# Two PSUM banks for attention's values and two for its scores, in place of one and three

## The chip, the core and the metric

The kernel runs on one core of a Trainium2 chip. The metric is the device time of one execution in microseconds (us); lower is better. Three runs of the kernel before gave a median of 904.16 us (903.74 to 908.43).

## What is computed

Three layers follow each other: causal attention with a bias that decays with the distance, a gated feed-forward layer (here "moe"), and a mixer that works first across the positions and then across the channels.

```python
B, H, S, D = 4, 8, 576, 64               # batches, heads, positions, width of a head
scores = q @ k.T / sqrt(D) + minimum(-(cum[:, None] - cum[None, :]), 0)   # cum = cumsum(max(s, 0)); causal
attn   = softmax(scores) @ v
x      = attn as (B, S, 512)
xk, xr = mu_k * x + (1 - mu_k) * x_prev, mu_r * x + (1 - mu_r) * x_prev
x      = sigmoid(xr @ w_r) * (maximum(xk @ w_k, 0) ** 2 @ w_v)
u      = x + (maximum(x.T @ w_tok1, 0) @ w_tok2).T
out    = u + maximum(u @ w_ch1, 0) @ w_ch2
```

## The kernel before

Attention has three stages. **early** (L302) takes the first 256 queries of the eight heads of batch 0. **late** (L348) takes the remaining 320 queries of these heads, with `late_pv` (L375) for their values. The 24 **visits** are the heads of batches 1 to 3, one visit a head, each with `scores` (L267), `transposes` (L389) and `values` (L427). Early and late multiply in plain fp32; the visits split each number into two fp32r parts.

All three go through the same steps for a block of 128 queries. TensorE (PE) multiplies queries and keys into a **score tile** `s` in PSUM (L308; L358; L277 and L278, which add two halves). VectorE (DVE) reads this tile once, adds the mask, writes it to SBUF as `P` and keeps the row's extremum `mx` (L252); from then on the score tile's bank is free. ScalarE (ACT) takes the exponential (L262), DVE the reciprocal of the sum (L263, L264), GpSimd (POOL) scales (L265). PE transposes `P` into a tile `t` (L316, L367, L399), which ACT and DVE copy out as `T`, `PF` or `PT`. PE multiplies that with the values into a **values tile** `pv` in PSUM (L326, L385, L447), which leaves by a copy on DVE (L77) in early and late, and in a visit by a copy on ACT (L453, into `tmp`) and an addition on DVE (L454, into `xt`). A block of 64 queries over 576 keys needs two score tiles of 288 columns. A visit has two values tiles, one for the first 256 queries (from `PF`) and one for the other 320 (from `PT`). The score tiles number 16, 32 and 144 in the three stages.

The feed-forward layer runs beside attention as units of 12 or 24 matmuls (`h` by `up` L467, `r` by `gate` L482, `vd` by `down` L494, all recorded at L109), so that PE has other work while a block waits for DVE, ACT and POOL. Their tiles have two PSUM banks of their own, `ps_d`. The weights are loaded as `raw` (L543) and split on ACT, DVE and POOL (L75, L555 to L561). From 455 us on the rest of the feed-forward layer and the mixer (`c`, `t`, `yn`) run alone.

No order is written out by hand. Each piece has a place (`at(...)`), and a scheduler lays the instructions of every engine in one fixed order when the program is built, from the places and from its own timeline, in which a tile can only be written once a bank of its pool is free. On the chip each engine then works through its own row and waits at its head. SyncE (SP) issues most transfers, also in such a row. PSUM has 8 banks: `ps_d` two, and during attention

```python
        ps_s = att.enter_context(tc.tile_pool(name="ps_s", bufs=3, space=PSUM, reuse_waits="tile"))
        ps_t = att.enter_context(tc.tile_pool(name="ps_t", bufs=2, space=PSUM, reuse_waits="tile"))
        ps_v = att.enter_context(tc.tile_pool(name="ps_v", bufs=1, space=PSUM, reuse_waits="tile"))
```

(L119 to L121). So score tile n uses the bank of tile n-3 and waits for its L252, and every values tile waits until the one before it has been read out.

Of the kernel before, what the change touches and what calls it, by code (L numbers as in the profile page):

```python
# [15 lines left out]
PSUM = bass.MemoryType.PSUM  # L16
# [8 lines left out]
def attention_moe_mixer(  # L25
# [86 lines left out]
    att = ExitStack()  # L112
    with tc.using_default_side("right"):
        qk_p = att.enter_context(tc.tile_pool(name="qk", bufs=1, reuse_waits="tile"))
        p_p = att.enter_context(tc.tile_pool(name="p", bufs=1, reuse_waits="tile"))
        pt_p = att.enter_context(tc.tile_pool(name="pt", bufs=1, reuse_waits="tile"))
        v_p = att.enter_context(tc.tile_pool(name="v", bufs=1, reuse_waits="tile"))
        st_p = att.enter_context(tc.tile_pool(name="st", bufs=6))
        ps_s = att.enter_context(tc.tile_pool(name="ps_s", bufs=3, space=PSUM, reuse_waits="tile"))  # L119
        ps_t = att.enter_context(tc.tile_pool(name="ps_t", bufs=2, space=PSUM, reuse_waits="tile"))  # L120
        ps_v = att.enter_context(tc.tile_pool(name="ps_v", bufs=1, space=PSUM, reuse_waits="tile"))  # L121

    HL = qk_p.tile([128, 4 * S], F32, name="HL")
    VS = v_p.tile([128, NS, 2 * D], F32, name="VS")
# [813 lines left out]
```

## Time and profile before

| | us |
|---|---|
| median of three runs (lowest to highest) | 904.16 (903.74 to 908.43) |
| the profiled execution | 905.17 |
| its span, first to last instruction | 903.4 |
| PE busy in the span | 861.6 |
| DVE, ACT, POOL busy | 515.1, 464.8, 318.5 |

The profile is of one execution. PE and PEld are TensorE's matmuls and its weight loads, which overlap; each matmul here has a weight load of its own. An engine's idle time is put down to what ended it.

### The profile page before, as it was taken

What the parts mean: (1) busy time and instruction counts of PE and PEld (TensorE: products, weight loads), DVE (VectorE), ACT (ScalarE), POOL (GpSimd) and SP (SyncE); (2) the same over time, 40 slices, a digit from 0 to 9 for tenths busy, and PEclk for the clock granted to TensorE, in tenths of its full rate; (3) what the DMA queues carried; (4) which work ended last, traced back from release to release, by engine and by line L of the source; (5) the groups of instructions that cost most, each with busy time, mean ns of one, the idle gap of its engine ahead of it and who ended that gap; (6) DMA issues with size and microseconds to landing.
All of it is one profiled execution on the core that took longest, in us unless ns stands there. A gap on an engine that the chain in (4) does not pass through costs nothing.

```text
span 903.4 us, 16007 instructions
## 1 busy us (share of the span) xinstructions
PE 861.6 (95%) x5456; PEld 789.6 (87%) x5456; DVE 515.1 (57%) x1542; ACT 464.8 (51%) x1264; POOL 318.5 (35%) x463
## 2 busy tenths in 40 slices
PE   6679999999899999999999998999999999999998
PEld 4335678998789989989989998999999999999998
DVE  5687786777898587876657865871331212212120
ACT  4787876766786756758456774760320201112010
POOL 4555535644564535655144764550000000000000
PEclk9759999999999999999999999999999999999999
DMA  7973345456654336542032656564022020211100
GB/s 168 215 193 89 88 124 133 98 122 152 139 117 107 88 81 142 121 108 48 29 118 78 216 160 200 183 180 129 24 75 66 18 79 27 63 43 53 36 1 36
DMA packets 65089, 93.69 MB, mean 104 GB/s; under 512 B 7424, under 2 KB 45568, under 8 KB 65008
## 3 DMA queue, kind: packets, MB, share of 16 engines
q1 hardware_dynamic: 58560, 77.00, 33.1%
q0 software_dynamic: 4576, 15.08, 5.5%
q10 hardware_dynamic: 1872, 0.59, 0.3%
q8 instruction: 43, 0.70, 0.3%
q14 instruction: 38, 0.31, 0.1%
HBM read 56.11 MB, written 14.75 MB: 78 GB/s over the span
## 4 chain that ended last, share of the span: by engine, by line
PE 77%; DMA 8%; DVE 7%; ACT 3%; issue 2%; POOL 2%; SPq 0%; ACTq 0%; POOLq 0%; DVEq 0%
PE c L109 33%; PE vd L109 9%; PE h L109 9%; PE r L109 5%; PE t L109 5%; PE pv L447 4%; PE t L399 3%; PE s L358 3%; PE s L277 2%; PE pv L385 2%; PE s L278 2%; DMA X<-HL 2%; DMA raw<-in_moe_w_k_dram 1%; PE t L367 1%; DVE raw L556 1%
## 5 line engine op out<-in xcount | busy, mean ns | idle before, releaser
L784 ACT ACTIVATE HID<-c 128x384 fp32r<-128x384 f32 x72 | 35.4, 491 | 220.6 <-PE c L109 220.5
L265 POOL TENSOR_SCALAR P<-P,sum 64x576 f32<-64x576 f32 (+4 forms) x160 | 106.5, 670 | 113.9 <-DVE sum L264 58.5
L109 PE MATMUL h<-XK,WK 128*128 128x256 f32 (+1 forms) x768 | 122.9, 301 | 3.6 <-DVE XK L465 1.5
L109 PE MATMUL vd<-KK,WV 128*128 128x256 f32 (+1 forms) x768 | 119.3, 299 | 0.0
L109 PEld LDWEIGHTS h<-XK,WK 128*128 128x128 f32 x768 | 105.6, 188 | 7.9 <-DVE XK L465 2.1
L262 ACT ACTIVATE P<-P,mx 64x576 f32<-64x576 f32 (+4 forms) x160 | 95.8, 600 | 30.7 <-DVE mx L252 26.7
L109 PEld LDWEIGHTS vd<-KK,WV 128*128 128x128 f32 x768 | 105.8, 188 | 2.2 <-ACT raw L555 0.4
L109 PE MATMUL c<-HID,WV 128*128 128x384 f32 x576 | 104.9, 336 | 0.0
L109 PE MATMUL c<-U,WK 128*128 128x384 f32 x576 | 104.2, 337 | 0.5 <-DVE HID L785 0.5
L109 PEld LDWEIGHTS c<-U,WK 128*128 128x128 f32 x576 | 99.9, 188 | 1.1 <-DVE HID L785 0.8
L109 PEld LDWEIGHTS c<-HID,WV 128*128 128x128 f32 x576 | 100.7, 188 | 0.0
L252 DVE CUSTOM_DVE_ANT_0 P<-s,maskc 64x288 f32<-64x288 f32 (+4 forms) x160 | 75.0, 474 | 26.3 <-PE t L399 6.9
L785 DVE SCALAR_TENSOR_TENSOR HID<-c,HID 128x384 fp32r<-128x384 f32 x72 | 40.0, 556 | 87.0 <-ACT HID L784 86.9
L842 DVE TENSOR_TENSOR ut<-c,ut 128x384 f32<-128x384 f32 x24 | 13.4, 558 | 124.1 <-PE c L109 124.1
L477 POOL TENSOR_TENSOR KK<-k,KK 128x256 fp32r<-128x256 f32 (+1 forms) x64 | 54.1, 848 | 31.5 <-ACT k L476 31.2
L109 PE MATMUL r<-XR,WR 128*128 128x320 f32 (+1 forms) x384 | 60.0, 298 | 0.0
L556 DVE SCALAR_TENSOR_TENSOR raw<-raw 128x256 int32<-128x256 int32 (+2 forms) x85 | 47.1, 556 | 19.6 <-ACT raw L555 15.7
L75 ACT ACTIVATE raw<-raw 128x256 f32<-128x256 f32 (+2 forms) x101 | 46.9, 465 | 19.6 <-DMA raw<-in_moe_w_v_dram 6.6
L399 PE MATMUL t<-ident,P 128*128 128x128 f32 (+1 forms) x360 | 53.6, 262 | 2.1 <-DVE PT L425 1.6
L109 PE MATMUL c<-HID,WR 128*128 128x384 f32 x288 | 54.2, 336 | 0.0
L109 PEld LDWEIGHTS r<-XR,WR 128*128 128x128 f32 x384 | 53.0, 188 | 0.7
L109 PE MATMUL c<-U,C1A 128*128 128x384 f32 x288 | 52.9, 343 | 0.0
(111 smaller groups left out, 1627.6 us busy)
## 6 DMA issues: line engine op xcount, KB each, us to landing
X<-HL SPq DMA_DIRECT2D x72, 288.0 KB
raw<-in_moe_w_ch_dram POOLq DMA_DIRECT2D x48, 256.0 KB, 3.3
HL<-in_qk_dram SPq DMA_DIRECT2D x12, 576.0 KB
ut<-u_d SPq DMA_DIRECT2D x32, 192.0 KB
yt<-y_d SPq DMA_DIRECT2D x16, 288.0 KB
u_d<-yt SPq DMA_DIRECT2D x16, 288.0 KB
raw<-in_moe_w_k_dram SPq DMA_DIRECT2D x8, 512.0 KB
raw<-in_moe_w_v_dram SPq DMA_DIRECT2D x16, 256.0 KB
```

Source lines behind the costliest of these rows:

```text
L75: nc.scalar.activation(out=out, in_=in_, func=AF.Copy, scale=scale)
L109: nc.tensor.matmul(ps, a, b, start=first and i == 0, stop=last and i == n - 1)
L252: nc.vector.tensor_tensor_reduce(out=P[0:m, c0:c1], in0=ps[0:m, 0:c1 - c0], in1=maskc[0:m, 512 - q0 + c0:512 - q0 + c1], scale=-scale, sca ...
L262: nc.scalar.activation(out=P[0:m, 0:w], in_=P[0:m, 0:w], func=AF.Exp, bias=mx[0:m, x:x + 1], scale=-1.0, accum_out=sm[0:m, 0:1])
L265: nc.gpsimd.tensor_scalar(out=P[0:m, 0:w], in0=P[0:m, 0:w], scalar1=sm[0:m, 1:2], scalar2=1.0, op0=ALU.mult, op1=ALU.mult)
L358: nc.tensor.matmul(ps[0:m, 0:c1 - c0], x[0:D + 4, 0, q0:q0 + m], x[0:D + 4, 1, c0:c1], start=True, stop=True)
L399: nc.tensor.transpose(ps[0:r, p0 + m * k:p0 + m * k + m], P[0:m, 128 * k:128 * k + r], ident[0:m, 0:m])
L447: nc.tensor.matmul(ps[:, o:n], vv[0:r, k, :], pair[t], start=(k == 0 and t == 0), stop=(k == nk - 1 and t == 1),)
L477: nc.gpsimd.tensor_tensor(out=kk[:, 1, m, 0:n], in0=t[:, 0:n], in1=f32(kk[:, 0, m, 0:n]), op=ALU.subtract)
L556: nc.vector.scalar_tensor_tensor(out=low, in0=high, scalar=3, in1=low, op0=ALU.logical_shift_left, op1=ALU.bitwise_or)
L784: nc.scalar.activation(out=hi, in_=ps, func=AF.Relu)
L785: nc.vector.scalar_tensor_tensor(out=lo, in0=ps, scalar=0.0, in1=f32(hi), op0=ALU.max, op1=ALU.subtract)
```

## The change

Two numbers of buffers: the pool of the score tiles goes from 3 to 2, the pool of the values tiles from 1 to 2. The sum stays 8 banks, and no instruction is added or taken away.

```diff
-        ps_s = att.enter_context(tc.tile_pool(name="ps_s", bufs=3, space=PSUM, reuse_waits="tile"))
+        ps_s = att.enter_context(tc.tile_pool(name="ps_s", bufs=2, space=PSUM, reuse_waits="tile"))
         ps_t = att.enter_context(tc.tile_pool(name="ps_t", bufs=2, space=PSUM, reuse_waits="tile"))
-        ps_v = att.enter_context(tc.tile_pool(name="ps_v", bufs=1, space=PSUM, reuse_waits="tile"))
+        ps_v = att.enter_context(tc.tile_pool(name="ps_v", bufs=2, space=PSUM, reuse_waits="tile"))
```

Score tile n now waits for the L252 of tile n-2, a values tile for the one two before it. Since the scheduler lays its rows by free banks, the rows of all five engines come out anew (on PE 1390 rows of equal instructions before, 1422 after). Three places follow, in the rows as they stand.

Place A is SP's row at the end of the early stage, as a difference. `X_425`, `X_428`, `X_431` and `X_434` are the operands of the first four late heads, loaded from `in_qk_dram` and from `ext_d` (the bias).

```order
 L337 DMA X_431<-in_qk_dram 64x1152
 L343 DMA VV_437<-in_v_dram 128x4x128
 L344 DMA VV_437<-in_v_dram 64x128
-L337 DMA X_434<-in_qk_dram 64x1152
 L343 DMA VV_440<-in_v_dram 128x4x128
-L344 DMA VV_440<-in_v_dram 64x128
 L338 DMA X_425<-ext_d 4x1152
 L338 DMA X_428<-ext_d 4x1152
 L338 DMA X_431<-ext_d 4x1152
+L344 DMA VV_440<-in_v_dram 64x128
+L543 DMA raw<-in_moe_w_v_dram 128x2x256 x2
+L208 DMA HL<-in_qk_dram 128x2x576
```

The load of the fourth head's operand and the second part of a value load went behind the first three biases, which so moved up by two transfers. Transfers from SP take eight semaphores in turn, so each waits until the one eight before it has landed: the first bias used to wait for the `raw` of row L543 that was issued sixth, and now waits for the one issued fifth.

Place B is PE's row at the turn from the first visit (`X_1348`) to the second (`X_1350`). Before:

```order
L399 MATMUL t<-ident,P_1603 128x128
L109 MATMUL h<-XK,WK 128x320
L385 MATMUL pv<-PT_1472,VV_1157 64x320 x3
L385 MATMUL pv<-PT_1472,VV_1157 64x192
L385 MATMUL pv<-PT_1472,VV_1157 64x64
L277 MATMUL s<-X_1348 64x288
L278 MATMUL s<-X_1457 64x288
L109 MATMUL h<-XK,WK 128x320 x6
L399 MATMUL t<-ident,P_1616 128x128 x2
L277 MATMUL s<-X_1350 128x128
L278 MATMUL s<-X_1597 128x128
```

and now, at the same place:

```order
L399 MATMUL t<-ident,P_1616 128x128 x2
L109 MATMUL h<-XK,WK 128x320 x4
L277 MATMUL s<-X_1348 64x288
L278 MATMUL s<-X_1457 64x288
L277 MATMUL s<-X_1348 64x288
L278 MATMUL s<-X_1457 64x288
L447 MATMUL pv<-PF,VV_1502 128x256 x2
L447 MATMUL pv<-PF,VV_1502 128x128 x2
L109 MATMUL h<-XK,WK 128x320 x2
L277 MATMUL s<-X_1350 128x128
L278 MATMUL s<-X_1597 128x128
```

The tile of 128 columns now waits for the first of the two tiles of 288, and 8 matmuls stand between them.

Place C is PE's row in a later visit, where the values tile from `PT` is filled and the one from `PF` of the next visit follows. Before:

```order
L277 MATMUL s<-X_1350 64x288
L278 MATMUL s<-X_1597 64x288
L447 MATMUL pv<-PT_1675,VV_1502 128x64
L399 MATMUL t<-ident,P_3401 128x128 x3
L447 MATMUL pv<-PT_1676,VV_1502 128x64
L399 MATMUL t<-ident,P_3436 128x128 x4
L109 MATMUL r<-XR,WR 128x256 x24
L277 MATMUL s<-X_1350 64x288
L278 MATMUL s<-X_1597 64x288
L277 MATMUL s<-X_1348 128x128
L278 MATMUL s<-X_1457 128x128
L447 MATMUL pv<-PF,VV_1797 128x256 x2
```

and now:

```order
L447 MATMUL pv<-PT_1676,VV_1502 128x192
L109 MATMUL r<-XR,WR 128x256 x10
L447 MATMUL pv<-PF,VV_1797 128x256
L109 MATMUL r<-XR,WR 128x256 x2
L447 MATMUL pv<-PF,VV_1797 128x256
L447 MATMUL pv<-PF,VV_1797 128x128 x2
L399 MATMUL t<-ident,P_3401 128x128 x3
L447 MATMUL pv<-PT_1675,VV_1502 128x64
L277 MATMUL s<-X_1350 128x512
L278 MATMUL s<-X_1597 128x512
L447 MATMUL pv<-PT_1676,VV_1502 128x64
```

The next visit's tile from `PF` is now filled while the one from `PT` is still open; before, 32 matmuls other than values stood between the two. Counted along PE's whole row in the visits, by the number of matmuls between a tile's first and the last one into its bank before it:

| in the visits | tiles | fewer than 10 | fewer than 15 | fewer than 20 |
|---|---|---|---|---|
| score tiles, before (bank of n-3) | 144 | 1 | 4 | 12 |
| score tiles, now (bank of n-2) | 144 | 7 | 20 | 31 |
| values tiles, before (bank of n-1) | 47 | 1 | | 4 |
| values tiles, now (bank of n-2) | 46 | 0 | | 0 |

Of the 32 late score tiles, 8 had fewer than 15 before and 15 have now. Counted against the values tile just before it, whatever its bank, 1 of 47 visit tiles began within 10 matmuls before, and 13 do now.

## Rows read from the trace of the kernel before

**Rows 1.** The page's first part: each engine's busy us, share of span and instructions.
```profile
PE 861.6 (95%) x5456; PEld 789.6 (87%) x5456; DVE 515.1 (57%) x1542; ACT 464.8 (51%) x1264; POOL 318.5 (35%) x463
```

**Rows 2.** Windows by stage: stretch, length, busy us of each engine, granted clock, DMA share, GB/s.
```profile
0.00:40.70 40.70, 24.68 (x78) 15.19 (x79) 23.71 (x99) 22.63 (x58) 19.09 (x47) 0.92 0.86 184
40.70:75.00 34.30, 27.61 (x75) 12.24 (x76) 26.98 (x70) 26.65 (x65) 21.50 (x19) 0.65 0.69 185
75.00:150.00 75.00, 74.36 (x470) 54.89 (x469) 57.49 (x189) 55.25 (x164) 33.09 (x45) 1.00 0.39 102
150.00:455.00 305.00, 296.12 (x2111) 274.24 (x2110) 228.74 (x822) 213.77 (x595) 158.16 (x225) 0.99 0.45 105
455.00:903.40 448.40, 438.86 (x2727) 433.04 (x2726) 178.15 (x364) 146.47 (x385) 86.66 (x129) 0.99 0.29 90
```

**Rows 3.** PE's waits up to 70 us: who waited for whom, us in total, times, longest.
```profile
PE s L358 <- DVE mx L252: 4.8, 2, 2.9
PE s L358 <- DMA X<-ext_d: 3.5, 1, 3.5
```

**Rows 4.** PE's waits from 150 to 456 us, the visits.
```profile
PE s L277 <- DVE mx L252: 2.0, 5, 0.8
PE pv L447 <- DVE xt L454: 1.9, 3, 0.9
```

**Rows 5.** The waits of TensorE's weight loads, 150 to 456 us.
```profile
PEld s L277 <- DVE mx L252: 3.7, 8, 1.1
...
PEld pv L447 <- DVE xt L454: 3.3, 6, 1.2
...
PEld pv L447 <- DVE PT L425: 0.8, 2, 0.6
...
PEld pv L447 <- ACT PT L424: 0.5, 2, 0.3
```

**Rows 6.** Groups by line: shapes and count, busy us and mean ns, idle before.
```profile
L252 DVE CUSTOM_DVE_ANT_0 P<-s,maskc 64x288 f32<-64x288 f32 (+4 forms) x160 | 75.0, 474 | 26.3 <-PE t L399 6.9 <-PE s L278 5.5 <-PE t L316 4.0
```

**Rows 7.** PE's timeline at a turn between visits: start us, us, engine, line, instruction, idle before.
```profile
217.34 0.39 PE L277 MATMUL s<-X 128*128 128x512 f32 x1
217.57 0.40 PE L278 MATMUL s<-X 128*128 128x512 f32 x1
...
220.61 0.29 PE L277 MATMUL s<-X 128*64 128x288 f32 x1
...
221.81 0.33 PE L277 MATMUL s<-X 128*128 128x128 f32 x1 [0.78 <-DVE mx L252]
```

**Rows 8.** DVE's timeline at the same place.
```profile
219.83 1.33 DVE L77 CAST VV<-VS 64x128 fp32r<-64x128 f32 x1
221.08 0.67 DVE L252 CUSTOM_DVE_ANT_0 P<-s,maskc 128x512 f32<-128x512 f32 x1
221.69 0.07 DVE L252 DVE_READ_ACCUMULATOR2_ANT mx<- 128x1 f32 x1
```

**Rows 9.** Windows of 5 us around 60 us, columns as in group 2.
```profile
55.00:60.00 5.00, 1.93 (x8) 0.85 (x7) 5.00 (x12) 5.00 (x14) 2.12 (x3) 0.77 0.98 180
60.00:65.00 5.00, 3.30 (x5) 1.20 (x6) 5.00 (x17) 3.86 (x9) 1.88 (x1) 0.50 0.13 41
```

**Rows 10.** PE's timeline at the start of the late stage.
```profile
36.69 0.48 PE L316 MATMUL t<-ident,P 128*128 128x128 f32 x1
40.70 4.48 PE L358 MATMUL s<-X 68*128 68x384 f32 x6 [3.54 <-DMA X<-ext_d]
```

**Rows 11.** SP's timeline, place A: start us, us to issue, transfer.
```profile
28.51 0.47 SPq L337 DMA_DIRECT2D X<-in_qk_dram  x1
29.87 0.37 SPq L343 DMA_DIRECT2D VV<-in_v_dram  x1
30.29 0.51 SPq L344 DMA_DIRECT2D VV<-in_v_dram  x1
33.77 4.79 SPq L338 DMA_DIRECT2D X<-ext_d  x4
```

**Rows 12.** SP's own waits: the one at the first bias.
```profile
SPq L338 <- DMA raw<-in_moe_w_k_dram: 3.0, 1, 3.0
```

## The prediction

> **What bounds the kernel now.** I read the page's first part first: PE is busy 861.6 of 903.4 us, DVE 515.1, ACT 464.8 [rows 1]. PE sets the time, and it has 41.8 us of idle time in all, so no wait that goes can be worth more than its part of that. The windows by stage come next, since a mean hides where the idle time lies [rows 2]: 16.0 us in the first 40.7 us (early stage, transfers at 0.86 of the DMA engines), 6.7 us from 40.7 to 75, 0.6 us from 75 to 150, 8.9 us in the 305 us of the visits, 9.5 us after attention has ended. The change touches PSUM tiles of attention alone. The last stretch keeps its instructions and its banks, and I count it at nothing.
>
> Then I looked up who makes PE wait in the visits, for the two kinds of tile that the change speaks of. For the bank of the values tile PE waits 1.9 us in 3 waits [rows 4], its weight loads 3.3 us in 6 [rows 5]. For the bank of a score tile it waits 2.0 us in 5 [rows 4], the weight loads 3.7 us in 8 [rows 5]. The two kinds of wait are of one size, and both are small. I price by the weight loads: each matmul has one ahead of it that cannot be taken while the matmul's bank is held, and the page's busy time of a matmul reaches into the wait behind it.
>
> Two more places matter. At 40.7 us PE has sat 3.54 us until the bias of the first late head landed [rows 10], and from 55 to 65 us DVE is busy without a break while PE works 5.2 us of 10 [rows 9]: there DVE is the bound, and PE's two waits for score tiles, 4.8 us [rows 3], are DVE's work seen from PE.
>
> **A bank more for the values.** The wait for L454 goes: no values tile of a visit now begins within 20 matmuls of the last one into its bank, where 4 did. I take the weight loads' whole 3.3 us off [rows 5]; by the matmuls' own waits it would be 1.9 [rows 4]. Early and late show no wait of PE for a values bank, so nothing is won there.
>
> What is late next? The products themselves. The second bank lets the scheduler put a values tile right behind the one before it (place C), as soon as it reckons the transposed block to be out. 13 of 47 tiles now begin within 10 matmuls of their predecessor, 1 did. Such a tile waits for data where it used to wait for a bank: its `PF` or `PT` must have left PSUM through ACT and DVE. The trace has four such waits, 0.8 us for L425 and 0.5 us for L424, 0.33 us each [rows 5]. Twelve more tiles at 0.33 us are 3.9 us; none if ACT and DVE are in time. I take 2.0 us, the middle, since nothing in the rows is nearer to one end.
>
> **A bank less for the scores.** A score tile is held from its first matmul until DVE has read it. The read itself takes 474 ns in the mean [rows 6], but DVE takes its work in order, and what stands ahead of the read counts too. One turn between visits shows it. The tile of 512 columns was multiplied at 217.57 us and begun to be read at 221.08, behind a CAST of 1.33 us, with the read's last part starting at 221.69 [rows 7, 8]. With three banks the next two tiles went in between, and PE waited 0.78 us at the third, at 221.81 [rows 7]. With two banks the second of these tiles, at 220.61, would have had to wait for that read: some 1.1 us, and the third, for the read of a tile multiplied still later.
>
> How often will this happen? The scheduler has spread the score tiles out, but not to the old distance. In the visits 20 of 144 now begin within 15 matmuls of the last one into their bank, against 4; within 20 it is 31 against 12. 305 us for 2111 matmuls are 0.144 us a matmul [rows 2], so 15 matmuls are 2.2 us and 20 are 2.9 us: less than the 3.5 us from the multiplication to the read at the turn above. In the trace 8 weight loads waited, 0.46 us each [rows 5], which is more than the 4 tiles under 15 and fewer than the 12 under 20. So I let each of the 16 tiles that are new under 15 wait, at 0.46 us: 7.4 us. The low end goes by the matmuls' own waits, 2.0 us over 12 tiles or 0.17 us a tile [rows 4], for 19 new tiles under 20: 3.2 us. The high end gives each of these 19 the longest wait seen, 1.1 us [rows 5]: 20.9 us. The value is near the low end because a wait also lets DVE, busy 229 of 305 us there [rows 2], catch up.
>
> In the late stage 7 tiles are new under 15. At 0.46 us they are 3.2 us, but PE was idle for only 0.6 us of the 75 behind the DVE-bound stretch [rows 2]; I take 1.0, ends 0 and 3.2. In the early stage the tighter tiles lie beside transfers, and PE waits for a transfer at its end [rows 10]: nothing.
>
> **SP's row, place A.** The first late bias was issued at 33.77 us [rows 11], after 3.0 us of waiting for the sixth `raw` [rows 12]. SP had stood ahead of the fourth operand until 28.51 [rows 11], and that load is now behind the biases, which wait for the fifth `raw` instead. The issue can then come after the VV load of 29.87 [rows 11], some 3 us earlier, and the late stage can begin up to 3.5 us earlier, which is PE's whole wait [rows 10]. What is late next is the work of DVE between 55 and 65 us [rows 9], which an earlier start reaches only in part. I take 2.0 us off, ends 0 and 3.5.
>
> **The sum.** Scores 7.4 and 1.0, data of the values 2.0; values bank -3.3, earlier start -2.0: +5.1 us, that is 910.3 on the profiled execution of 905.17. That execution lies 1.0 us over the median of 904.16, by which the result will be told, so I predict 909.3.
>
> The Trainium skill speaks against this sign (Perfetto Trace Analysis, Matmuls): independent groups of matmuls should rotate through different PSUM banks, so that one is emptied while the next is computed. The values had no rotation and get one, the scores keep one of two. By that rule the 3.3 us come back and the scores' price is nothing; the rows bear out the first half, while the scores' own waits with three banks [rows 5] speak against the second.
>
> **The rivals.** *Slower by much.* DVE's lateness, not the distance, sets the waits: reads stand behind CASTs and splits as at 221.08 [rows 8], and each of the 16 new tiles pays 1.1 us, 17.6 in place of 7.4. With the other terms the sum is 15.3, 919.5 us. It decides as soon as reads come over 2.2 us after their matmuls as a rule. For it: the 3.5 us at that turn. Against it: with three banks only 8 of 144 tiles waited.
>
> *The two wishes cancel.* The scheduler leaves just as much room as the chip needs. Scores 3.2, values -3.3, start -2.0, no wait for data: -2.1, 902.1 us. For it: all waits are small and PE has other units to put between. Against it: the distances did shrink.
>
> *Faster.* The earlier start carries through. PE's 3.5 us go whole, and half of the 6.7 us that it is idle from 40.7 to 75 [rows 2], 3.3, because DVE's block begins earlier and less falls together; with values -3.3 and scores 3.2 the sum is -6.9, 897.3 us. In that stretch the granted clock was 0.65 in the mean [rows 2], a mix of both levels, after a stretch in which PE had sat waiting; a start without that wait could give some of it back too. Against it: DVE at 5.00 of 5.00 twice over [rows 9] does not get shorter.
>
> That the rows stay as they were, so that the number does nothing, is ruled out by places A to C.
>
> **How the numbers follow.** Less than 0.5%, 4.5 us, is about what a measurement of this kernel cannot tell from no change; so faster ends at 899.6 and slower begins at 908.7. My forecast has 0.42, the much slower case 0.18, the cancelling 0.25, the faster 0.15. The forecast with its inner bounds (the data's wait 0 to 3.9, the late tiles 0 to 3.2) spreads over some 905 to 914, of which I lay 0.6 above 908.7: 0.25, and with 0.18 that is 0.43 slower. The faster case and a little of the cancelling one make 0.18 faster; 0.39 is left for the same. The range leaves about a tenth on either side: from 898.5, within the faster case, to 920, just above the much slower one's time.
>
> **What would show it.** The wait of `pv` for L454 is gone from PE's waits in the visits, and waits of `pv` for L424, L425, L408 or L409 have grown to some 3 us. The waits of `s` for L252 in the visits rise from 3.7 us on the weight loads to about 11, in over 20 waits. The first L358 begins near 38 us, with its wait for `ext_d` under 2 us. The stretch after attention keeps its length within 2 us, and attention ends some 5 us later than 455. I am wrong if the waits of `s` stay under 5 us, if DVE's read order moved with the tiles so that a read follows its matmul within 2 us, or if the transfers of the first 75 us, reordered at more places than A, gain or lose more than the 3.5 us.

## The result and the profile after

The changed kernel takes 916.73 us, the median of 7 runs (913.31 to 919.76); the kernel before, run beside it, 906.23 us (903.74 to 910.63). The ratio is 1.0109, with a 95% interval of 1.0084 to 1.0135: slower by 1.1%. The profiled execution after took 913.87 us, 8.7 more than the one shown of before. It is one of the shortest of the seven, so what the two traces account for is 8.7 us, while the medians lie 10.5 us apart.

First the page's engine line of after and its windows by stage, the columns as in [rows 2]. The visits now end near 463 us, so the last two stretches are cut there.

```profile
PE 871.3 (96%) x5456; PEld 793.8 (87%) x5456; DVE 518.5 (57%) x1542; ACT 462.7 (51%) x1264; POOL 323.9 (36%) x463
```
```profile
0.00:40.70 40.70, 31.25 (x84) 18.20 (x84) 26.27 (x105) 24.71 (x64) 19.85 (x47) 1.00 0.88 220
40.70:75.00 34.30, 28.13 (x75) 12.41 (x74) 28.51 (x72) 29.40 (x72) 22.47 (x19) 0.95 0.53 143
75.00:150.00 75.00, 72.91 (x463) 54.32 (x462) 55.80 (x181) 49.93 (x147) 35.58 (x45) 1.00 0.38 99
150.00:463.00 313.00, 300.95 (x2117) 277.98 (x2116) 227.50 (x824) 213.38 (x599) 158.46 (x225) 0.98 0.44 101
463.00:912.10 449.10, 438.06 (x2724) 430.92 (x2722) 180.42 (x364) 145.25 (x386) 87.53 (x129) 1.00 0.29 90
```

Count the matmuls up to 150 us, first of before, then of after:

```profile
0.00:150.00 150.00, 126.65 (x622) 82.32 (x623) 108.19 (x358) 104.54 (x285) 73.67 (x110) 0.90 0.59 143
```
```profile
0.00:150.00 150.00, 132.29 (x619) 84.92 (x620) 110.58 (x357) 104.03 (x281) 77.91 (x110) 0.99 0.55 142
```

With 622 against 619 next to nothing is lost up to there. But PE is idle for 17.7 us in place of 23.4, and busy for 5.6 us more with as many matmuls: what it saved in waits it lost in longer matmuls. The visits then take 313.0 us in place of 305.0, and the rest 449.1 in place of 448.4. The 8.0 us of the visits have two parts. PE's idle time is 313.00 - 300.95 = 12.05 us against 8.88, 3.2 more. Its busy time is 4.8 longer, of which the 6 more matmuls at 0.144 us account for 0.9. So some 3.9 us, an estimate, went into matmuls that took longer.

Next, who makes PE and its weight loads wait between 150 and 464 us; compare [rows 4, 5].

```profile
PE s L277 <- DVE mx L252: 4.3, 6, 2.0
PE pv L447 <- ACT PF L408: 2.1, 1, 2.1
...
PE pv L447 <- DVE PF L409: 1.0, 1, 1.0
```
```profile
PEld s L277 <- DVE mx L252: 6.4, 9, 2.3
...
PEld pv L447 <- ACT PF L408: 2.7, 2, 2.4
...
PEld pv L447 <- DVE PF L409: 1.5, 3, 1.1
...
PEld pv L447 <- DVE PT L425: 0.9, 2, 0.6
PEld pv L447 <- ACT PT L424: 0.7, 2, 0.4
```

The wait of `pv` for L454 is gone. In its place `pv` waits for data, 2.7 + 1.5 + 0.9 + 0.7 = 5.8 us on the weight loads, where before had 1.5: the 1.3 of [rows 5] and one wait more, which stands further down in the same answer.

```profile
PEld pv L447 <- ACT PF L408: 0.2, 1, 0.2
```

The waits of `s` rose from 3.7 to 6.4.

Laid over the trace of before at equal work done, after falls back mostly at two places: at 171.6 us, where PE waits 2.02 us for a score bank, and around 222 to 239 us. Here is PE's timeline at the first (columns as in [rows 7]), then the second, as the timeline of PE and of ACT.

```profile
171.59 0.33 PE L277 MATMUL s<-X 128*128 128x128 f32 x1 [2.02 <-DVE mx L252]
```

```profile
222.43 0.34 PE L278 MATMUL s<-X 128*128 128x384 f32 x1
224.85 0.39 PE L447 MATMUL pv<-PF,VV 128*128 128x256 f32 x1 [2.08 <-ACT PF L408]
```
```profile
222.46 1.26 ACT L75 ACTIVATE HL<-HL 128x576 fp32r<-128x576 f32 x2 [3.34 <-DMA HL<-in_qk_dram]
223.62 0.71 ACT L262 ACTIVATE P<-P,mx 128x512 f32<-128x512 f32 x1
224.24 0.18 ACT L262 ACTIVATION_READ_ACCUMULATOR P<-P,mx 128x1 f32 x1
224.33 0.47 ACT L408 ACTIVATE PF<-t 128x384 fp32r<-128x384 f32 x1
```

ACT stands for 3.34 us before the split of the next pair of heads, because its load has not landed, and the exp and the `PF` that PE needs are queued behind. Before had the same stand, 3.17 us at the turn of 208 to 212, and PE did not notice. It had units of the feed-forward layer (the `vd` rows) laid there. Both engines of before at that turn:

```profile
211.81 1.26 ACT L75 ACTIVATE HL<-HL 128x576 fp32r<-128x576 f32 x2 [3.17 <-DMA HL<-in_qk_dram]
```
```profile
208.12 2.37 PE L109 MATMUL vd<-KK,WV 128*128 128x320 f32 x15
...
212.40 1.28 PE L109 MATMUL vd<-KK,WV 128*128 128x320 f32 x7
```

In after no row of a unit stands between 221.7 and 229 us. And the clock fell. The windows below are first of before, then of after; the last three numbers of a row are the granted clock, the DMA share and GB/s.

```profile
225.00:228.40 3.40, 3.40 (x13) 2.92 (x11) 2.07 (x13) 1.74 (x6) 2.02 (x4) 0.50 0.84 171
228.40:239.00 10.60, 8.92 (x53) 6.64 (x54) 9.16 (x34) 8.62 (x23) 5.81 (x9) 1.00 0.53 129
```
```profile
225.40:228.40 3.00, 2.86 (x10) 2.07 (x10) 2.77 (x13) 2.92 (x11) 3.00 (x4) 0.50 0.98 194
228.40:239.00 10.60, 9.60 (x40) 8.27 (x41) 5.64 (x26) 5.03 (x15) 4.28 (x8) 0.50 0.63 133
```

After its wait PE ran at 0.50, the 1.2 GHz level, for 13.6 us; before for 3.4 near the same time. In the 10.6 us from 228.4 the one did 40 matmuls, the other 53. By the busy time of one there (0.240 against 0.168 us) that stretch holds some 2.9 of the 3.9 us of longer matmuls; it is an estimate, since they are not the same matmuls. Behind the first stop, of 2.02 us, the clock did not fall:

```profile
170.00:180.00 10.00, 7.77 (x51) 7.15 (x52) 8.07 (x23) 8.98 (x27) 9.25 (x12) 1.00 0.45 90
```

### The profile page after: what moved, and what is told of

Its sections match the earlier page's. It is cut to its first block, busy times and chain, and to the rows that moved or that the text cites. A ratio compares the mean times of both kernels' runs of the same rounds, so it can differ in the third digit from the quotient of the medians.

```text
span 912.1 us, 16017 instructions
## 1 busy us (share of the span) xinstructions
PE 871.3 (96%) x5456; PEld 793.8 (87%) x5456; DVE 518.5 (57%) x1542; ACT 462.7 (51%) x1264; POOL 323.9 (36%) x463
## 5 line engine op out<-in xcount | busy, mean ns | idle before, releaser
L265 POOL TENSOR_SCALAR P<-P,sum 64x576 f32<-64x576 f32 (+4 forms) x160 | 106.2, 668 | 133.1 <-DVE sum L264 68.6
L252 DVE CUSTOM_DVE_ANT_0 P<-s,maskc 64x288 f32<-64x288 f32 (+4 forms) x160 | 75.8, 475 | 27.4 <-PE s L278 10.7
L109 PE MATMUL r<-XR,WR 128*128 128x320 f32 (+1 forms) x384 | 63.9, 301 | 1.3 <-ACT k L474 1.3
L399 PE MATMUL t<-ident,P 128*128 128x128 f32 (+1 forms) x360 | 55.6, 272 | 2.9 <-POOL P L265 1.4
L557 DVE SCALAR_TENSOR_TENSOR raw<-raw 128x256 int32<-128x256 int32 (+2 forms) x85 | 56.9, 672 | 1.2
L556 DVE SCALAR_TENSOR_TENSOR raw<-raw 128x256 int32<-128x256 int32 (+2 forms) x85 | 47.1, 556 | 18.2 <-ACT raw L555 14.6
L277 PE MATMUL s<-X 128*128 128x128 f32 (+1 forms) x144 | 48.9, 342 | 4.4 <-DVE mx L252 4.3
```

The costliest lines, as they stand in the source:

```text
L109: nc.tensor.matmul(ps, a, b, start=first and i == 0, stop=last and i == n - 1)
L252: nc.vector.tensor_tensor_reduce(out=P[0:m, c0:c1], in0=ps[0:m, 0:c1 - c0], in1=maskc[0:m, 512 - q0 + c0:512 - q0 + c1], scale=-scale, sca ...
L265: nc.gpsimd.tensor_scalar(out=P[0:m, 0:w], in0=P[0:m, 0:w], scalar1=sm[0:m, 1:2], scalar2=1.0, op0=ALU.mult, op1=ALU.mult)
L277: nc.tensor.matmul(ps[0:m, 0:c1 - c0], x1[:, 0, q0:q0 + m], x1[:, 1, c0:c1], start=True, stop=False)
L399: nc.tensor.transpose(ps[0:r, p0 + m * k:p0 + m * k + m], P[0:m, 128 * k:128 * k + r], ident[0:m, 0:m])
L556: nc.vector.scalar_tensor_tensor(out=low, in0=high, scalar=3, in1=low, op0=ALU.logical_shift_left, op1=ALU.bitwise_or)
```

## The experiments

I had two theories. *Banks*: PE waits for the scores' two banks, the new order is secondary. *Order*: the scheduler lays out another order for any number of banks, and what costs is how that order fits the rest. A third, narrower one concerned ACT's stand. Several runs fix the order: every engine is told, instruction by instruction, to keep the row of another kernel (`ORDER` is that row, one list for each engine).

```diff
+    for rows in ORDER.values():
+        ...
+        for a, b in zip(names, names[1:]):
+            tc.add_manual_dep(tc.nc.find_inst_by_name(b), a,
+                mybir.DependencyInfo(mybir.DependencyClass.NoSync, mybir.DependencyReason.DATA), reason="order")
```

**Order and banks crossed.** Run e1 has the banks of before (three and one) with the order of after.

> The banks of before (three for scores, one for the values) with the order of after: on every engine the instructions stand as after has them, up to attention's end; only at 8 places, where one values bank makes that order impossible, PE takes matmuls of other units ahead of a values tile. If the loss lies in the order itself, whatever the banks, this stays near after, 8 to 12 us over before (914 to 918). If it lies in PE waiting for the scores' two banks, the third bank takes it back: 0 to 3 us over before (904 to 908), with the data waits of the values left.

Run e2 has the banks of after (two and two) with the order of before.

> The banks of after (two and two) with the order of before on every engine; at 13 places PE takes other matmuls ahead of a score tile that would otherwise stand for ever. If the order is the cause, this is near before, within 3 us (904 to 909). If the banks are, it is at least as slow as after, 914 to 925, since this order reckoned with three banks: waits of s for the read of L252 then grow from 3.7 us on the weight loads to over 10.

Measured: e1 940.53 us, 1.0366 of before (1.0319 to 1.0412); e2 953.08, 1.0494 (1.0442 to 1.0545). Each crossing is much slower than both kernels, which neither theory had. PE's waits from 150 to 490 us, the largest row of e1 and then of e2:

```profile
PE pv L447 <- DVE xt L454: 28.8, 18, 4.8
```
```profile
PE s L277 <- DVE mx L252: 31.8, 30, 4.0
```

So two score banks are dear to an order that counts on three (30 waits of 1.1 us in the mean), and one values bank is dear to an order that counts on two. By making a new order the scheduler takes back most of it: 953 became 917. In e1, where scores had three banks, no wait of `s` is left in the visits, and it is slow all the same. A bank number and its order cannot be judged apart.

**ACT's stand.** In ACT's row the copies of each split stand 6 instructions later, in POOL's row the subtractions 3 later; all else as in after (e3) or before (e4). One split of e3, ACT's row:

```diff
-L75 ACTIVATE HL<-HL 128x576 x2
 L262 ACTIVATE P_1660,sum<-P_1660,mx 128x384
 L262 ACTIVATE P_1679,sum<-P_1679,mx 128x512
 ...
 L464 ACTIVATE XR<-t 128x320
+L75 ACTIVATE HL<-HL 128x576 x2
```

> The changed kernel, same order on all engines but for one thing: in ACT's row the two copies of each split of HL in the visits stand 6 instructions later, in POOL's row its four subtractions 3 later. ACT then no longer stands for 2 to 4 us in front of the load of HL with the exps and the PF behind it. If the loss at 169 and at 222 us comes from that stand, which two score banks no longer bridge, 5 to 9 us come back (908 to 912). If it comes from the two banks anywhere, or from the order elsewhere, no more than 2 us come back (915 to 919).

> The same two moves in the rows of the kernel before. If three score banks bridge ACT's stand, as its trace seems to show, there is little to win: 0 to 2 us under before (904 to 907). If PE pays for ACT's stand with three banks as well, 4 us or more come back (902 or less), and the stand does not tell the two kernels apart.

Measured: e3 920.96 us, 1.0138 (1.0095 to 1.0181); e4 920.37, 1.0138 (1.0099 to 1.0177). So e4 is 1.4% slower than the kernel that it comes from, and e3 cannot be told from after (1.0084 to 1.0135): the 5 to 9 us did not come back. The largest of PE's waits in e3, 150 to 490 us:

```profile
PE t L399 <- POOL P L265: 10.8, 6, 3.7
```

The stand moved from ACT to POOL, whose subtractions wait for ACT's copies and hold the `P` of L265 behind them. So this did not take the stand away, and it does not decide the theory. It shows that the load is waited for in two rows at once.

**Is it one lucky order?** The place of the feed-forward units (the expectations say: of the mixer) is moved from 3 to 2.8 and to 3.2, in both kernels; with the original that makes three pairs, each with orders of its own.

```diff
-            with at(N0 + n + 3):
+            with at(N0 + n + 2.8):   # e5 and e6; 3.2 in e7 and e8
```

> The kernel before with one place moved a little: the units of the mixer beside attention stand at 2.8 behind their item in place of 3, so that the scheduler lays out another order with the same banks. It is one half of a pair with the next run. If the banks cost something in any order, this is near before (903 to 911) and the next run 6 to 13 us over it. If the 10 us are the luck of one order, the two befores with moved units already differ from before by 5 us and more, and the pairs differ in both directions.

> The changed kernel with the same move to 2.8. Banks cost in any order: 6 to 13 us over its pair. Luck of the order: anything from 6 us under it to 12 over it, with no likeness to the other pairs.

> The kernel before with the units at 3.2 in place of 3. Banks cost in any order: near before, 903 to 911. Luck of the order: off by 5 us or more in either direction.

> The changed kernel with the units at 3.2. Banks cost in any order: 6 to 13 us over its pair. Luck of the order: no likeness to the other two pairs, and the sign may turn.

| units at | 3 and 1 banks, us (ratio to before) | 2 and 2 banks, us (ratio) | last values matmul, us | from it to the end, us |
|---|---|---|---|---|
| 3 | 906.23 | 916.73 (1.0109) | 453.3, 461.4 | 450.1, 450.7 |
| 2.8 | 916.85 (1.0130) | 923.59 (1.0208) | 464.8, 468.1 | 449.0, 452.5 |
| 3.2 | 906.29 (1.0008) | 918.10 (1.0135) | 456.5, 464.2 | 447.1, 453.6 |

The last two columns come from each profiled execution, 3 and 1 banks first. Both theories have something. A place moved by 0.2 made the kernel before 1.3% slower (0.9 to 1.7%), so the luck of an order is as large as the whole change. Yet in all three pairs 2 and 2 is the slower, by 0.8 (1.0208 / 1.0130), 1.1 and 1.3%. The visits end 3.3 to 8.1 us later, and the stretch behind them is 0.6 to 6.5 us longer. In part the waits repeat too. PE's waits in e6, 130 to 466 us:

```profile
PE s L277 <- DVE mx L252: 4.7, 6, 2.3
PE pv L447 <- ACT PF L408: 3.0, 2, 2.7
PE pv L447 <- ACT PT L424: 2.9, 5, 1.8
```

Its pair e5 has 1.7 us for the first, none for the second, 1.3 for the third, and 3.2 for L454, which e6 does not have. In e8 and e7 the first is 3.0 and 1.9 us.

**Half of the change.** Two banks for scores, one for the values, the eighth idle.

```diff
-        ps_s = ... name="ps_s", bufs=3
+        ps_s = ... name="ps_s", bufs=2
```

> One half of the change alone: two banks for scores, one for the values, the eighth bank left idle; the scheduler makes its own order for it. If the lost bank of the scores is the cause, this is as slow as after or slower, since the wait for L454 comes back: 914 to 921. If the second bank of the values is, by products that start ahead of their data, this is near before: 904 to 909.

Measured: 909.87 us, 1.0037 (1.0012 to 1.0062). Neither expectation, but nearer to the second. PE's waits, 130 to 466 us:

```profile
PE pv L447 <- ACT PT L424: 3.3, 3, 1.8
PE r L109 <- ACT k L474: 2.5, 3, 1.1
...
PE pv L447 <- DVE xt L454: 0.9, 2, 0.6
...
PE s L277 <- DVE mx L252: 0.6, 2, 0.4
```

With two score banks, as in after, `s` waits 0.6 us in 2 waits, less than with three (2.3 in 6 waits in the same window of before). With this order the bank taken from the scores costs some 0.4%. The other 0.7% of the change came with the bank that was given. The traces put it less simply: in e9 the last values matmul stands at 458.5 us, 5.2 later than in before and 2.9 earlier than in after, but the stretch behind it is 448.2 us long, the shortest of the three.

**Is it the second values bank itself?** Run e12 has the banks of after and, to the end of the program, the order of e9.

> The banks of after (two and two) with the order of e9 on every engine, to the end of the program: the one thing that differs from e9 is that the values have their second bank, the one thing that differs from after is the order. If the second bank costs by the order that the scheduler makes with it, this is e9's time less its waits for L454 (0.9 us): 0 to 2 us under e9, 1 to 4 us over before (907 to 911). If something in the second bank itself costs on the chip, it is near after (914 to 919). A ratio to before under 0.998 would make it a version that beats both.

Measured: 910.95 us, 1.0060 (1.0038 to 1.0082). The wait for L454 is gone, and the time is that of e9 within the intervals: the bank brings nothing measurable, nor does it harm. Against after only the order differs. With the ratio of after above, the intervals just part (1.0082 and 1.0084); with that of its repetition below they overlap (from 1.0060). The runs themselves do not overlap, though they were not taken side by side: 909.41 to 912.45 us for e12, 912.54 to 919.97 for after in both. So the order which the scheduler makes with the second bank costs some 0.4% more than that of e9. Where it costs it the traces do not show, since the profiled executions of e12 and after lie only 1.7 us apart. That an order weighs as much as a bank is plain from e5 as well: e12, with two and two, is at 1.0060, e5, with three and one, at 1.0130.

**Values apart.** After's order, but in PE's row the values tiles that began within 10 matmuls of the one before stand behind up to 16 matmuls of other work, as here:

```diff
-L109 MATMUL h<-XK,WK 128x320 x12
+L109 MATMUL h<-XK,WK 128x320 x9
+L447 MATMUL pv<-PF,VV_1502 128x256 x2
+L447 MATMUL pv<-PF,VV_1502 128x128 x2
+L109 MATMUL h<-XK,WK 128x320 x3
```

> The changed kernel with the order of after, except that in PE's row no values tile of the visits begins within 10 matmuls of the last matmul of the values tile before it (13 did; 1 is left within 15): its matmuls stand behind up to 16 matmuls of other work. All other engines keep their rows. If the waits of pv for PF and PT, 5 to 6 us in the trace of after, are lost time, 3 to 6 us come back (911 to 914). If the scores' two banks hold PE anyway, it stays at 915 to 919, and the waits turn up as waits of s or t.

Measured: 925.42 us, 1.0187 (1.0156 to 1.0218), slower than after and outside both expectations. At the turn of 222 us PE stops again, for another tile. PE's timeline of e10, then POOL's:

```profile
227.23 0.34 PE L278 MATMUL s<-X 128*128 128x384 f32 x1
230.82 0.65 PE L399 MATMUL t<-ident,P 128*128 128x128 f32 x3 [3.25 <-POOL P L265]
```
```profile
228.66 1.54 POOL L222 TENSOR_TENSOR HL<-HL 128x288 f32<-128x288 f32 x2 [4.41 <-ACT HL L75]
230.18 0.58 POOL L265 TENSOR_SCALAR P<-P,sum 128x384 f32<-128x384 f32 x1
```

The wait of `pv` for `PF` was not lost time of its own. Whatever tile stands there waits until the split's load has landed. This stop is 1.2 us longer than that of after and so explains only a part of the 8.7 us between the two; PE's idle time in the visits is 17.2 us in place of 12.1, and the clock stood at 0.50 there for 20.5 us in place of 13.6; why both grew stays open. In before the feed-forward units covered the time of the stand; that they would do it here too is read from the rows, not run.

**The same kernel again.**

> The changed kernel once more, for a second trace. If the stops at 171.6 and 224.9 us (2.0 and 2.1 us) and the stretch of half clock behind the second (13.7 us) belong to its order, they are there again, within 1 us and within 4 us of length. If they are chance, the trace loses its time elsewhere and the total still comes to 913 to 920.

Measured: 917.51 us, 1.0094 (1.0060 to 1.0128). The second stop is there again, 2.45 us long; the first is not (the same tile waits 0.28 us, at 168.25), though e10, with the same rows up to there on the other engines, has it with 2.11 us at 174.5. PE's timeline, then windows behind the stop:

```profile
221.77 0.39 PE L447 MATMUL pv<-PF,VV 128*128 128x256 f32 x1 [2.45 <-ACT PF L408]
```
```profile
224.00:228.00 4.00, 2.58 (x11) 1.56 (x11) 2.15 (x11) 1.90 (x5) 4.00 (x7) 0.50 0.84 191
228.00:234.10 6.10, 5.95 (x25) 5.21 (x25) 3.76 (x19) 3.08 (x10) 1.59 (x3) 0.54 0.65 128
```

So the stop at 222 us and the slow clock behind it (here some 10 us) belong to this order, while the score wait at 171.6 us comes in some executions only.

## Why the prediction came out as it did

The sign was right, and 916.73 lies within 898.5 to 920; the point of 909.3 was 7.4 us low, of which 2.1 are the base (906.23 beside this run, 904.16 when the forecast was made). That the number fell so near is in part luck: the largest term was 4.7 us too high, and 3.9 us came from one that was missing. The result is nearer to the much slower rival's 919.5, but did not come by its mechanism.

**The scores' waits, forecast 7.4, measured 2.7** (3.7 to 6.4, in 9 waits where I had over 20). That is below the low end of 3.2, and it was 1.8 in e11, the second trace of the same kernel (5.5 us, 150 to 462 us). The 6.4 are little over the 5 us under which I had called myself wrong. The step that failed is that each of the 16 new tiles under 15 matmuls would wait. What the forecast held fixed moved: the time from the start of a score tile's last matmul (L278) to the start of DVE's read of it. Matched by order and shape over the 144 tiles of the visits, it is 2.2 us in the median before and 1.2 after, 2.0 and 2.3 in e5 and e7, 1.1 in e6 and e8, 1.3 in e9. That is one of the signs that I had named for being wrong. A distance in matmuls says little when the reads come nearer too; e9 has PE's waits down to 0.6 us. For the same reason the much slower rival fails: it takes 1.1 us a tile, and e2 shows just that, 31.8 us in 30 waits, but for the old order with the new banks, which nobody runs. Where I had counted nothing, in the early stage, PE waits 2.2 us in 4 waits (`s` of L308 for L252); before had none there.

**The values bank, forecast -3.3, measured -3.3**: the wait for L454 is gone. **The data of the values, forecast 2.0, measured 4.3** (1.5 to 5.8; 6.3 in e11), above the high end of 3.9. The trace had five such waits, not the four that I priced. I spread 0.33 us over twelve tiles; it came as one wait of 2.4 us, one of 1.1 and small ones. The mean price of a wait missed where the wait lies: at the turn, behind ACT's stand. And e10 shows that even this term is not a cost of its own.

**PE's idle time in the visits** should have grown by 7.4 + 2.0 - 3.3 = 6.1 us and grew by 3.2. That the total still came out higher is a **term that the sum did not have**: matmuls at half clock behind the stop, most of some 3.9 us. It is no mark of two and two: e9 and e12 ran at half clock for as long in their visits (3.4 and some 10.2 us), with a loss of 0.4 and 0.6%.

**The earlier start, forecast -2.0, measured about 0.** Its first half came as foretold. SP issues the bias at 28.65 us, and the first L358 begins at 36.47 us without a wait, against [rows 10, 11]. PE's timeline and SP's:

```profile
36.47 3.36 PE L358 MATMUL s<-X 68*128 68x384 f32 x4
```
```profile
28.65 1.07 SPq L338 DMA_DIRECT2D X<-ext_d  x3
```

But 619 matmuls by 150 us against 622 leave nothing of it (e11, the same kernel, has 628, 6 more than before, or 0.9 us). The step that failed here is that a wait which goes is time won. PE's idle time up to 150 us did fall by 5.6 us, and the matmuls took it back: up to 75 us the values matmuls of the early stage (L326, 128x256) took 658 ns in the mean in place of 592. In before the clock is on record at 1.00 from 27.0 to 33.8 us; after has no record there, but its 658 ns are near the 648 of its matmuls of this shape from 41 to 65 us. The waits of `s` for L252 in the late stage rose from 4.8 us in 2 [rows 3] to 5.9 in 6. With the late tiles' 1.0 the two terms make -1.0 forecast, 0 measured. So the faster rival fell: the 3.5 us came, and did not carry through, and longer matmuls took where that rival had the clock give.

**The stretch after attention, counted at nothing**, is 0.6 us longer here; in the other two pairs it is 3.5 and 6.5. That step held for this order only.

**The cancelling rival** had the scores' price right, 3.2 for 2.7, but no wait for data and no clock. With the measured terms, 2.7 + 4.3 - 3.3 + 0 + 3.9 + 0.6, the sum is 8.2 of the 8.7 us between the two traces.

The Trainium skill's rule that groups of matmuls should rotate through different PSUM banks (Perfetto Trace Analysis, Matmuls) was the argument on the other side. These runs agree with it only in that the wait for L454 went (3.3 us on the weight loads). The values got their rotation and the kernel lost 1.1%; e9, with no rotation for the values and one of two for the scores, lost 0.4%.

What stays open: why the orders for two values banks leave the turns and the end less well covered in all three pairs. The pairs show that they do: PE's idle time in the visits is 2.0 to 3.2 us longer, and behind them 1.2 to 3.0. At one turn the traces show how. Open too is what e9 loses 0.4% by. Whether another planner's rule would cover them was not tried. No version beat the kernel before.

## What to carry to other kernels

Where a scheduler makes the order, a number of buffers is not a resource with a price of its own: keep the order fixed once and the banks fixed once, and try neighbouring orders, before calling a bank good or bad. Price a wait by where it lies, at a turn with every other engine late or among work that covers it, not by a mean over tiles. And look at TensorE's clock behind a new wait: it took as much again at one place and nothing at another.

## What the runs showed of the hardware that was not expected

A stop of 2.08 us (2.45 in e11) was followed by 13.6 us (some 10) at 0.50, while before, with a stop of 0.78 us at 221.81, the half clock lasted 3.4 us. Here the second effect of a wait was as large as the first. But it is no price of a wait of that length. Behind the 2.02 us at 171.6 in after the clock stayed at 1.00, and so it did behind 2.12 us at 216.7 in e2. Behind attention both kernels stop for 2.1 us (at 474.0 before, at 480.5 after), and there the half clock lasted 3.4 us in both. What decides the length stays open.

The granted clock of a window can read 1.00 where there is no record of it. The first record of before comes at 27 us, that of after at 65 us; from there on the records have no gap. The next rows are the transposes of one shape in after, first from 41 to 65 us, then from 80 to 130 (busy us, then mean ns of one):

```profile
L367 PE MATMUL t<-ident,P 128*128 128x128 f32 x7 | 1.7, 421 | 0.0
...
L367 PE MATMUL t<-ident,P 128*128 128x128 f32 x31 | 5.3, 278 | 0.0
```

421 against 278 ns, much as in before (409 against 274), where the clock at that place reads 0.77 and 0.50 [rows 9]. So from 41 to 65 us after ran at the lower level, as before did for most of that time, and the mean clock of the whole run, higher in after (0.988), tells nothing of it.
